# A gated linear recurrence before a squared-relu layer: four edits to the order of a planned kernel

## The chip, the core and the metric

The kernel runs on one core of a Trainium2 chip. Its engines are TensorE (PE, matmuls), VectorE (DVE), ScalarE (ACT), GpSimd (POOL) and SyncE (SP); each has its own queue and works it off in order, and DMA transfers are issued from the queues of SP, ACT and POOL. The metric is the device time of one execution in microseconds.

## What is computed

```python
scale = np.minimum(mag, 0.999) / (mag + 1e-06)      # mag = |a|
for t in range(S):                                   # S = 768, D = 48, 4 batches x 8 heads
    new_re = ar * S_re - ai * S_im
    new_im = ar * S_im + ai * S_re
    S_re, S_im = (new_re + kv, new_im)               # kv = outer(k_t, v_t)
    y[:, :, t] = np.einsum('bhd,bhde->bhe', q[:, :, t], S_re)
x = y.transpose(0, 2, 1, 3).reshape(B * S, H * D)    # 3072 x 384
g = np.maximum(x @ w_in, 0.0) ** 2                   # 384 x 2048
out = g @ w_out                                      # 2048 x 384
```

A complex state of 48 x 48 per batch and head decays by a normalised complex gate at each step, takes in a product of k and v, and is read by q. The result, head by head in a row of 384, goes through two matrices with a squared relu between them.

## The kernel before

The 3072 tokens are worked in six blocks n = 0 to 5 of 512 tokens. A batch has 768 tokens, so blocks 0 and 3 begin with a fresh state, blocks 1 and 4 cross from one batch to the next, and blocks 2 and 5 end one. Eight heads lie in two halves z = 0, 1 of four; a pair is two heads, so a block has four pairs, 0 and 1 in half 0, 2 and 3 in half 1.

Per block the code writes these steps, in functions of `fast_path`:

- `load` (L926): a_re, a_im, q, k of both halves into the tiles `aq0`, `aq1`. For block 0 the a_im parts are issued by ScalarE, a_re, q and k by SP, and half 0 of the gates comes in two parts (u = 0, 1); for the later blocks GpSimd issues all. When a half's gates have landed, GpSimd copies one element (L931) and from then on fetches weights (L821).
- `chain`: `roots` (squares L979/L984, sum L987, logarithm, exponential and square on ScalarE L989 to L994, a Newton step on VectorE L997, L1001), `normalise` (L1007 to L1021) and `inner` (products within four tokens, L1036 to L1041). For block 0 `joint` then turns and sums on TensorE with a permutation and its negative (L1111), and ScalarE copies the result to `e` (L1122, L1125). The negative, `nperm`, lives in the tile `yt0`; ScalarE writes it at L1072. Then VectorE scans over the chunks (L1197 to L1219), TensorE turns the result back (L1090), `factors` and `apply` give every token its own decay (L1129 to L1153, L1320 to L1367). The products of q and k with these factors are written into the tiles `f` (L1365). `gather` moves the K~ rows from there to `KC0` or `KC1` by DMA (L1409).
- `pairs`: for blocks 1 to 5, `turn` transposes f in 32 x 32 blocks on VectorE (L1449) and moves them by 12 DMAs per pair into a `QT` tile (L1454), four of them on ScalarE's queue and eight on SP's; for block 0 TensorE transposes instead (L1473) and ScalarE copies (L1476). `score` multiplies within a chunk on TensorE (L1495), and VectorE masks the result into an `A` tile (L1501; for block 1 also into `T`). `keep` makes chunk states from K~ and v on TensorE (L1525); VectorE copies those with no predecessor (L1535) and adds the others to the state before (L1537) in the tiles `St` and `S`. `mix` puts both together on TensorE (L1549, L1553) into one bank, ScalarE copies it to a `yt` tile (L1559), and SP moves it by DMA to `xT` (L1567).
- `dense`, in two groups of 256 tokens: first matrix (L1609), relu and square on ScalarE (L1641, L1642), second matrix (L1656 in block 0, then L1718 in a form with seven products and additions by VectorE, L1733, L1742, and a copy by ScalarE, L1737).

The weights come as 64-bit floats and are converted in pieces by ScalarE (L834, L838) and VectorE (L840, L844, L847) between these steps in blocks 0 and 1. `sums_of_w2` (L1708) prepares sums of the second matrix for the form with seven products.

The order is set by a planner, the class `Plan`. Each step is added with its engine, an assumed duration, what it reads and writes and a rank; a DMA step has a size and an assumed latency too. `order` simulates: at each moment every engine takes the ready step with the lowest rank. `shift` adds offsets from two tables, by number of group and of step, to the ranks. `emit` writes the instructions in that order and, where it foresees TensorE waiting, fills the time with matmuls of the identity with itself (L739).

Of the kernel before, what the change touches and what calls it, by code (L numbers as in the profile page):

```python
# [632 lines left out]
def fast_path(ctx, tc, q, k, v, a_re, a_im, moe_w_in, moe_w_out, out, flag):  # L633
# [310 lines left out]
    def chain(n):  # L944
# [126 lines left out]
        if n == 0:  # L1071
            step("ACT", 0.25, [], [("yt", 0)], lambda: act.mul(out=nperm, in_=perm, mul=-1.0),  # L1072
                 rank)
        for fn in (roots, normalise, inner):
            for z in range(2):
                fn(z)

# [318 lines left out]
    def gather(n, z, p, np):  # L1396
# [5 lines left out]
        for i in needs(n):  # L1402
            for lo, hi, at in spans(i):
# [7 lines left out]
                    rank, (hi - lo) * np * 2 * R * 4, group=(n, p))  # L1411
# [14 lines left out]
    def pairs(n, which):  # L1426
# [9 lines left out]
        def turn(i):  # L1436
# [13 lines left out]
            for b in range(W):  # L1450
                for j in range(NJ):
# [4 lines left out]
                            in_=T6[32 * b:32 * b + 32, i % 2, j]), rank, 65536,  # L1456
# [49 lines left out]
        def keep(i):  # L1506
# [23 lines left out]

            def go2():
                for j in need:
                    o = new if j == 3 else at[j + 1]
                    if at[j] is None:
                        dve.tensor_copy(out=o, in_=ps[:, j])  # L1535
                    else:
                        dve.tensor_tensor(out=o, in0=ps[:, j], in1=at[j], op=ALU.add)  # L1537
            step("DVE", len(need) * (tt(2 * D) + 0.11) - 0.11, [(b,), ("S", n % 2, i)],
# [319 lines left out]
    for n in range(AFTER):  # L1858
        for j in range(3):
# [4 lines left out]
        groups={5: -99.15, 9: -3.76, 14: 438.99, 15: 438.99, 25: 104.57, 68: -227.0, 70: 100.43, 73:  # L1864
# [5 lines left out]
        single={11: -198.18, 14: 0.04, 51: -1.52, 52: 4.52, 58: -215.58, 96: 438.99, 143: 438.99,  # L1870
# [66 lines left out]
```

## Time and profile before

| | us |
|---|---|
| median of 3 runs (680.1 to 682.59) | 681.67 |
| profiled execution | 678.34 |
| its span, first to last instruction | 676.6 |
| TensorE busy | 656.4 |
| VectorE busy | 557.2 |
| ScalarE busy | 341.8 |
| mean granted TensorE clock | 0.994 of full |

A row of the timeline gives start, duration, engine, line, operation, the tile written and read, and in brackets the idle time just before and what ended it. ACTq and SPq are rows of a queue that issues DMAs; how long such a row lasts is how long the queue was held. A row of waits gives what waited for what: total, times, longest. A row of windows gives a stretch and its length, then busy time and instructions of PE, PEld, DVE, ACT and POOL, then the granted clock, the share of the DMA engines and GB/s.

### The profile page before, as it was taken

How to read it: one execution, taken by the hardware profiler on the slowest of the kernel's cores; microseconds unless marked ns; L12 is line 12 of the kernel's file. 1: busy time of each engine (PE TensorE's matmuls, PEld its weight loads, DVE VectorE, ACT ScalarE, POOL GpSimd, SP SyncE). 2: the span in 40 equal slices, each digit the busy share in tenths (PEclk: the TensorE clock that was granted, in tenths of full speed). 3: DMA queues.
4: the chain of work that ended last, by engine and by line, in shares of the span. 5: the costliest groups of instructions: out<-in, count | busy, mean ns of one | idle time of the engine just before them, and what ended most of it. 6: DMA issues, size and time to landing. Idle time of an engine off the chain costs nothing.

```text
span 676.6 us, 13669 instructions
## 1 busy us (share of the span) xinstructions
PE 656.4 (97%) x5194; PEld 593.0 (88%) x5194; DVE 557.2 (82%) x1153; ACT 341.8 (51%) x564; POOL 147.5 (22%) x247
## 2 busy tenths in 40 slices
PE   9989979999989999999999999999999999999996
PEld 9989868768768898998988998989899999989996
DVE  4999998899599999989998898999987995247641
ACT  5997588954366524557425639236548132132230
POOL 4400455033210012013133143031050110042100
PEclk9989999999989999999999999999999999999999
DMA  7941596235850018525156443166260264187600
GB/s 224 318 159 36 131 232 205 89 94 146 210 149 25 23 43 202 141 73 141 36 135 165 123 118 69 48 161 171 68 176 24 50 151 108 40 301 263 222 8 23
DMA packets 39492, 86.33 MB, mean 128 GB/s; under 512 B 8917, under 2 KB 16545, under 8 KB 39417
## 3 DMA queue, kind: packets, MB, share of 16 engines
q0 software_dynamic: 16576, 57.03, 29.9%
q1 hardware_dynamic: 17784, 22.20, 12.7%
q10 hardware_dynamic: 5056, 6.13, 3.5%
q8 instruction: 43, 0.70, 0.5%
q14 instruction: 33, 0.26, 0.1%
HBM read 48.76 MB, written 4.72 MB: 79 GB/s over the span
## 4 chain that ended last, share of the span: by engine, by line
PE 59%; DVE 8%; issue 1%; DMA 1%; ACT 1%; ACTq 0%; DVEq 0%
PE d L1609 26%; PE d L1718 23%; PE sc L1495 3%; PE yp L1549 2%; PE yp L1553 2%; PE tr L1525 2%; DVE g L1733 1%; DMA QT<-aq 1%; DVE T L1708 1%; DVE f L1365 1%; PE tr L1090 0%; DVE f L1036 0%; DVE KC L1217 0%; DVE aq L1449 0%; DVE aq L1067 0%
## 5 line engine op out<-in xcount | busy, mean ns | idle before, releaser
L1609 PE MATMUL d<-xT,w 128*128 128x256 f32 x1104 | 245.9, 380 | 2.9 <-DMA xT<-yt 2.1
L1609 PEld LDWEIGHTS d<-xT,w 128*128 128x128 f32 x1104 | 208.0, 190 | 32.5 <-DMA xT<-yt 2.5
L1641 ACT ACTIVATE g<-d 128x512 f32<-128x512 f32 x92 | 54.7, 595 | 180.5 <-PE d L1609 112.7
L1718 PE MATMUL d<-w,g 128*128 128x192 f32 x640 | 112.3, 328 | 1.6 <-ACT ot L1737 1.6
L1718 PEld LDWEIGHTS d<-w,g 128*128 128x128 f32 x640 | 104.4, 190 | 3.3 <-ACT ot L1737 2.1
L1718 PE MATMUL d<-T,g 128*128 128x192 f32 x480 | 85.3, 327 | 0.3 <-DVE g L1733 0.3
L1733 DVE TENSOR_TENSOR g<-g 128x512 f32<-128x512 f32 x80 | 54.2, 686 | 31.7 <-PE d L1718 17.0
L1718 PEld LDWEIGHTS d<-T,g 128*128 128x128 f32 x480 | 79.0, 190 | 1.5 <-DVE g L1733 0.6
L1642 ACT ACTIVATE g<-g 128x512 f32<-128x512 f32 x96 | 60.6, 631 | 3.1
L739 PE MATMUL d<-ident 128*128 128x128 f32 x502 | 59.7, 283 | 1.6 <-POOL ident masks.py:199 1.6
L739 PEld LDWEIGHTS d<-ident 128*128 128x128 f32 x502 | 58.9, 199 | 2.0 <-POOL ident masks.py:199 1.6
L1679 POOL DMA_DIRECT2D out_dram<-ot x22 | 12.5, 567 | 196.3 <-DVE ot L1742 184.9
L1449 DVE STREAM_TRANSPOSE aq<-f 128x768 f32<-128x768 f32 x40 | 47.9, 1266 | 0.2
L1559 ACT COPY yt<-yp 112x512 f32<-112x512 f32 x24 | 26.5, 1106 | 40.0 <-PE yp L1553 34.4
L1409 POOL DMA_DIRECT2D KC<-f x56 | 34.7, 626 | 53.0 <-issue 22.0
L1365 DVE TENSOR_TENSOR f<-aq 128x768 f32<-128x768 f32 (+1 forms) x56 | 44.3, 839 | 0.4
L1656 PE MATMUL d<-w,g 128*128 128x384 f32 x128 | 44.0, 491 | 0.3 <-DVE w L847 0.3
L1742 DVE TENSOR_TENSOR ot<-ot,d 128x192 f32<-128x192 f32 x70 | 23.6, 349 | 18.3 <-PE d L1718 17.7
L1495 PE MATMUL sc<-QT 96*64 96x64 f32 (+1 forms) x736 | 38.1, 252 | 0.0
L1656 PEld LDWEIGHTS d<-w,g 128*128 128x128 f32 x128 | 23.7, 190 | 15.3 <-DVE w L847 0.9
L1495 PEld LDWEIGHTS sc<-QT 96*64 96x64 f32 x736 | 35.0, 137 | 0.4 <-issue 0.2
L1036 DVE TENSOR_TENSOR f<-aq 128x768 f32<-128x768 f32 (+1 forms) x48 | 34.2, 755 | 0.6
(198 smaller groups left out, 955.5 us busy)
## 6 DMA issues: line engine op xcount, KB each, us to landing
QT<-aq SPq DMA_DIRECT2D x152, 64.0 KB, 2.2
f<-in_moe_w_in_dram POOLq DMA_DIRECT2D x8, 768.0 KB, 6.9
f<-in_moe_w_out_dram POOLq DMA_DIRECT2D x8, 768.0 KB, 6.9
QT<-aq ACTq DMA_DIRECT2D x76, 64.0 KB, 2.7
out_dram<-ot POOLq DMA_DIRECT2D x22, 192.0 KB, 3.1
KC<-f POOLq DMA_DIRECT2D x20, 192.0 KB, 4.3
xT<-yt SPq DMA_DIRECT2D x36, 96.0 KB, 2.3
T<-in_moe_w_out_dram POOLq DMA_DIRECT2D x4, 768.0 KB, 9.7
```

The source lines that it names most:

```text
L739: plan = Plan(lambda b: pe.matmul(bank[b][:, 0:C], lhsT=ident, rhs=ident, start=True, stop=True), ["d2", "d1", "d0"], lambda ap: tc.nc.val ...
L1036: dve.tensor_tensor(out=f, in0=x0, in1=x1[:, j].unsqueeze(1).to_broadcast(list(x0.shape)), op=ALU.mult)
L1365: lambda j=j, r=r, o=o: dve.tensor_tensor(out=o[:, :, :, r * D:(r + 1) * D], in0=qk[:, j], in1=a[:, r], op=ALU.mult), late[z])
L1409: lambda i=i, queue=queue, lo=lo, hi=hi, a0=a0, a1=a1: queue.dma_start(out=kc[lo:hi, i], in_=nat[a0:a1]),
L1449: lambda nat=nat, dst=dst, j=j: dve.transpose(out=dst[:, j], in_=nat), rank)
L1495: pe.matmul(sa[r:r + C // 2, j, :, lo:32], lhsT=T[:, j, 1, h, ts(late, C // 2)], rhs=T[:, j, 0, h].rearrange("p (c t) -> p c t", c=W)[:, : ...
L1609: pe.matmul(ps, lhsT=w1[:, f // FP, m, ts(f % FP, C)], rhs=xT[:, n % 2, m, ts(grp, G)], start=(m == 0), stop=(m == NM - 1))
L1641: act.activation(out=o, in_=ps, func=AF.Relu)
L1642: act.activation(out=o, in_=o, func=AF.Square)
L1656: pe.matmul(ps, lhsT=gt[:, f % 2, ts(i, C)], rhs=w2[:, f], start=(f == 0), stop=(f == NF - 1))
L1718: pe.matmul(bank[b][:, 0:DH], lhsT=g4[:, r, j], rhs=w(j), start=first and j == 0, stop=last and j == NT - 1)
L1733: step("DVE", tt(4 * C), gk(x0, h) + gk(x1, h), gk(o, h), lambda: dve.tensor_tensor(out=g4[:, o, sl], in0=g4[:, x0, sl], in1=g4[:, x1, sl] ...
```

## The change

Four edits:

1. In block 0 ScalarE's negation of the permutation is no longer written first in the chain, but behind `normalise` of half 0; it waits there for two columns of that half's `f`.
2. In `keep`, chunk states with no predecessor (16 copies, in blocks 0, 1, 3 and 4) are copied from the accumulator by ScalarE (L1533 of the new file) instead of VectorE. VectorE's additions now also wait for `St`, that is for these copies.
3. The planner counts 2.7 us instead of 1.8 for the landing of K~ rows, and 2.2 instead of 1.8 for that of QT.
4. The two tables of `shift` are replaced as a whole.

```diff
-        if n == 0:
-            step("ACT", 0.25, [], [("yt", 0)], lambda: act.mul(out=nperm, in_=perm, mul=-1.0),
-                 rank)
         for fn in (roots, normalise, inner):
             for z in range(2):
                 fn(z)
+                if n == 0 and z == 0 and fn is normalise:
+                    step("ACT", 0.25, key(0, 1), [("yt", 0)], lambda: act.mul(
+                        out=nperm, in_=perm, mul=-1.0), rank)
...
                         out=kc[lo:hi, i], in_=nat[a0:a1]),
-                    rank, (hi - lo) * np * 2 * R * 4, group=(n, p))
+                    rank, (hi - lo) * np * 2 * R * 4, 2.7, group=(n, p))
...
                             out=t[32 * j:32 * j + 32, b],
-                            in_=T6[32 * b:32 * b + 32, i % 2, j]), rank, 65536,
+                            in_=T6[32 * b:32 * b + 32, i % 2, j]), rank, 65536, 2.2,
...
+            begun = [j for j in need if at[j] is None]
+            for j in begun:
+                step("ACT", 0.27, [(b,)], [("St", s)], lambda j=j: act.copy(
+                    out=at[j + 1], in_=ps[:, j]), rank, group=(n, i))
+
             def go2():
                 for j in need:
-                    o = new if j == 3 else at[j + 1]
-                    if at[j] is None:
-                        dve.tensor_copy(out=o, in_=ps[:, j])
-                    else:
+                    if j not in begun:
+                        o = new if j == 3 else at[j + 1]
                         dve.tensor_tensor(out=o, in0=ps[:, j], in1=at[j], op=ALU.add)
-            step("DVE", len(need) * (tt(2 * D) + 0.11) - 0.11, [(b,), ("S", n % 2, i)],
+            step("DVE", (len(need) - len(begun)) * (tt(2 * D) + 0.11) - 0.11,
+                 [(b,), ("S", n % 2, i), ("St", s)],
...
-        groups={5: -99.15, 9: -3.76, 14: 438.99, 15: 438.99, 25: 104.57, 68: -227.0, 70: 100.43, 73:
+        groups={3: -342.38, 5: -305.58, 7: -355.32, 9: -326.37, 14: 448.38, 15: 448.29, 24: 1.52,
```

What this does to the order, at three places. The first is the start of ScalarE's queue in block 0; `yt_89` holds the negative permutation, `aq_68` and `aq_69` are the halves 0 and 1 of the gates, a DMA of 128x2x192 is one of the two parts of half 0. Before and then after:

```order
L667 ACT_TABLE_LOAD
L1072 ACTIVATE yt_89<-perm 128x128
L926 DMA aq_68<-in_a_im_dram 128x2x192 x2
L926 DMA aq_69<-in_a_im_dram 128x4x192
L979 ACTIVATE f_70<-aq_68 128x384 x2
```

```order
L667 ACT_TABLE_LOAD
L926 DMA aq_68<-in_a_im_dram 128x2x192
L926 DMA aq_69<-in_a_im_dram 128x4x192
L926 DMA aq_68<-in_a_im_dram 128x2x192
L979 ACTIVATE f_70<-aq_68 128x384
```

The negation is gone from the front, and the second part of half 0 has moved behind the whole of half 1. On VectorE, from the inner products of half 0 on (L1041), two L840, one L847 and one L1067 stood ahead of the last L1036 of half 1, which `joint` waits for, and now stand behind it.

The second place is VectorE in block 1, where the f of half 1 is done (L1365) and the first mix of the block needs its masks (L1501, into T and A_85) and its states (St_87). Before and then after; the additions of L1537 are L1540 in the new file:

```order
L1365 TENSOR_TENSOR f_71<-aq_69 128x4x4x48 x4
L1537 TENSOR_TENSOR St_87<-tr_112,S_84 96x96
L1535 COPY St_87<-tr_112 96x96
L1537 TENSOR_TENSOR S_83<-tr_112,St_87 96x96
L1501 TENSOR_TENSOR T<-sc_110,mask 128x512
L1501 TENSOR_TENSOR A_85<-sc_111,mask 128x512
L1449 STREAM_TRANSPOSE aq_69<-f_71 128x4x2x3x32 x4
```

```order
L1365 TENSOR_TENSOR f_71<-aq_69 128x4x4x48 x4
L1449 STREAM_TRANSPOSE aq_69<-f_71 128x4x2x3x32 x3
L1501 TENSOR_TENSOR T<-sc_110,mask 128x512
L1501 TENSOR_TENSOR A_85<-sc_111,mask 128x512
L1449 STREAM_TRANSPOSE aq_69<-f_71 128x4x2x3x32
L1540 TENSOR_TENSOR St_87<-tr_112,S_84 96x96
L1540 TENSOR_TENSOR S_83<-tr_112,St_87 96x96
```

Three of the four transposes of half 1 have moved ahead of the masks and the fourth ahead of the additions, and the copy has left the queue. Further on in this block, the masks of pair 2 have moved: one stands ahead of L997 and the other behind L1001, and both ahead of L1708, where they stood behind all of these and behind the state additions.

The third place is ScalarE in block 1, at the same time: QT_73 and QT_74 are the QT tiles of pairs 2 and 3, whose issues come from the transposes above; L964 to L1007 is the chain of the next block; L1559 is L1563 in the new file and L1641, L1642 are L1645, L1646. Before and then after:

```order
L1454 DMA QT_73<-aq_69 32x512 x4
L964 ACTIVATE f_70,sums<-aq_68 128x1536
L1559 COPY yt_89<-yp 112x4x4x32
L1454 DMA QT_74<-aq_69 32x512 x4
L989 ACTIVATE f_70<-f_70 128x768
L991 ACTIVATE f_70<-f_70 128x768
L994 ACTIVATE f_70,sums<-f_70 128x768
```

```order
L1454 DMA QT_73<-aq_69 32x512 x4
L1533 COPY St_87<-tr_112 96x96
L1645 ACTIVATE g<-d_109 128x512
L1646 ACTIVATE g<-g 128x512
L1645 ACTIVATE g<-d_107 128x512
L1646 ACTIVATE g<-g 128x512
L1454 DMA QT_74<-aq_69 32x512 x2
L1533 COPY St_88<-tr_113 96x96
L1454 DMA QT_74<-aq_69 32x512 x2
L964 ACTIVATE f_70,sums<-aq_68 128x1536
L1563 COPY yt_89<-yp 112x4x4x32
L989 ACTIVATE f_70<-f_70 128x768
```

The four issues of QT_74 have moved ahead of L964 and of the copy to yt, and the copies of the new states stand behind QT issues. Elsewhere: at the end of block 0 the K~ gathers of half 1 have moved ahead of block 1's loads on GpSimd and ahead of the xT moves on SP, `keep` of pair 3 stands before the mix of pair 2 on TensorE, and its state additions stand before the last masks on VectorE. In block 3 eight QT issues in a row stand before a relu on ScalarE, where there were five. The last rows of each engine are as before.

More of the change, by code (lines that the diff above doesn't have):

```diff
@@ L1863, in fast_path @@
     plan.shift(
-        groups={5: -99.15, 9: -3.76, 14: 438.99, 15: 438.99, 25: 104.57, 68: -227.0, 70: 100.43, 73:
[5 rows of a table removed]
-        single={11: -198.18, 14: 0.04, 51: -1.52, 52: 4.52, 58: -215.58, 96: 438.99, 143: 438.99,
[10 rows of a table removed]
+        groups={3: -342.38, 5: -305.58, 7: -355.32, 9: -326.37, 14: 448.38, 15: 448.29, 24: 1.52,
[7 rows of a table added]
+        single={3: 97.06, 11: -213.0, 44: 41.06, 48: -1.3, 49: 26.15, 53: 32.15, 63: 1.44, 65: 2.25,
[20 rows of a table added]
     with tc.manual_schedule():
```

42 rows, old and new, of tables (groups, single) are left out of this document.

## The prediction

> **What bounds the kernel now.** I read the page's first part, then the waits of TensorE, then the stages in which those waits lie.
>
> ```profile
> span 676.6 us, 13669 instructions
> PE 656.4 (97%) x5194; PEld 593.0 (88%) x5194; DVE 557.2 (82%) x1153; ACT 341.8 (51%) x564; POOL 147.5 (22%) x247
> ...
> L739 PE MATMUL d<-ident 128*128 128x128 f32 x502 | 59.7, 283 | 1.6 <-POOL ident masks.py:199 1.6
> ```
>
> TensorE is busy for 97% of the span, but 59.7 us of that is L739, the matmuls of the identity with itself that the planner puts into waits it foresees. They all lie in the first 95 us, before the first dense block, so the start is bounded by something else, and only from about 100 us on is TensorE the bound. The profiled execution took 678.34 us: 676.6 of span and 1.74 outside it. The sum below is made against it; the median of the runs shown, 681.67, lies 3.33 above it, and I carry that distance over unchanged.
>
> What is left of TensorE's time outside the start is in its waits (total, times, longest).
>
> ```profile
> PE yp L1549 <- DVE A L1501: 2.6, 2, 2.0
> PE d L1609 <- DMA xT<-yt: 2.1, 1, 2.1
> PE tr L1111 <- DVE f L1036: 1.7, 1, 1.7
> ...
> PE d L1718 <- ACT ot L1737: 1.6, 1, 1.6
> PE tr L1525 <- DMA KC<-f: 1.6, 2, 1.4
> PE d L1609 <- ACT g L1641: 0.8, 1, 0.8
> ```
>
> No wait is longer than 2.1 us. The waits for L1036, for KC<-f and for xT<-yt lie before 100 us. Those for A (L1501), for ot (L1737) and for g (L1641) lie behind, and each of those is lost for good, since nothing catches it up. Two of the waits cost more than their length. The stages by windows show it in the granted clock (the number ahead of the DMA share):
>
> ```profile
> 30.00:40.00 10.00, 8.26 (x82) 7.54 (x80) 9.76 (x14) 9.89 (x11) 1.76 (x3) 0.86 1.03 299
> ...
> 90.00:100.00 10.00, 6.57 (x107) 5.73 (x104) 9.11 (x15) 7.91 (x10) 3.41 (x6) 1.00 1.05 251
> ...
> 190.00:200.00 10.00, 9.65 (x116) 8.02 (x118) 9.16 (x15) 7.04 (x11) 2.04 (x3) 0.83 0.54 145
> ...
> 470.00:480.00 10.00, 8.38 (x92) 8.01 (x88) 9.30 (x15) 6.19 (x9) 0.80 (x2) 1.00 0.62 166
> ```
>
> The stages with the gaps of 1.71 us (34.5) and 1.95 us (188.3) lost 14% and 17% of 10 us, that is 1.4 and 1.7 us of full speed. The stages with gaps of 2.08 and 1.62 us kept 1.00. So a gap of this size throttles sometimes, and its price is its length or its length plus about 1.7.
>
> **The change, part by part: the start (0 to 100 us).** ScalarE's first rows are:
>
> ```profile
> 2.27 0.31 ACT L1072 ACTIVATE yt<-perm 128x128 f32<-128x128 f32 x1 [0.16 <-POOL perm L722]
> 2.27 2.43 ACTq L926 DMA_DIRECT2D aq<-in_a_im_dram  x3
> ...
> 6.82 0.56 DVE L984 TENSOR_TENSOR f<-aq 128x384 f32<-128x384 f32 x1 [5.33 <-DMA aq<-in_a_im_dram]
> ...
> 10.42 0.56 DVE L984 TENSOR_TENSOR f<-aq 128x384 f32<-128x384 f32 x1 [2.37 <-DMA aq<-in_a_im_dram]
> ```
>
> The table load ends at 2.10; the negation and the first a_im transfer start at 2.27, and VectorE then idles 5.33 and 2.37 us for a_im. With the negation gone from the front, the three issues can begin 0.17 us sooner. They also change places: the whole of half 1 goes ahead of the second part of half 0. The second part was needed at 10.42, and half 1 landed last, at 12.81:
>
> ```profile
> 12.81 0.22 POOL L931 COPY gate<-aq 128x1 f32<-128x1 f32 x1 [1.78 <-DMA aq<-in_a_im_dram]
> ...
> 29.54 0.55 DVE L840 TENSOR_SCALAR w<-KC 128x768 uint32<-128x768 uint32 x1
> ...
> 30.01 0.95 DVE L847 CUSTOM_DVE_ANT_0 w<-w,w 128x1536 uint16<-128x1536 uint16 x1
> ...
> 36.20 0.32 PE L1111 MATMUL tr<-perm,f 128*64 128x128 f32 x1 [1.71 <-DVE f L1036]
> ...
> 36.53 0.76 DVE L1067 TENSOR_TENSOR aq<-aq,f 128x576 f32<-128x576 f32 x1
> ```
>
> VectorE's order loses what stood ahead of the end of half 1's inner products (L1036, which released L1111 at 36.20): two L840, one L847 and one L1067 now stand behind it, 2 x 0.55 + 0.95 + 0.76 = 2.8 us. That is the most there is to gain. The other end: the queue carries the same bytes, so the part of half 0 that is now last may land when half 1 did, at 12.81, which is 2.4 us later than it was used; then 0.4 is left. The negation itself (0.31 us, now behind normalise of half 0) is first read by L1111, which waits for half 1's products anyway, and costs nothing as long as they end later. I take 2.0, nearer to VectorE's work, because in the rows its idle time ends at 11 us and from there to 36 us it has work.
>
> This reaches the first dense matmul only if the end of the start moves too:
>
> ```profile
> 91.84 1.28 DVE L1501 TENSOR_TENSOR A<-sc,mask 128x512 f32<-128x512 f32 x2
> ...
> 93.40 0.40 PE L1525 MATMUL tr<-v,KC 128*64 128x48 f32 x8 [1.35 <-DMA KC<-f]
> ...
> 95.27 0.65 PE L1549 MATMUL yp<-A,v 128*48 128x128 f32 x8
> ...
> 99.73 0.45 PE L1609 MATMUL d<-xT,w 128*128 128x256 f32 x1 [2.08 <-DMA xT<-yt]
> ```
>
> Block 0's last masks were done at 93.12. Its last mix began at 95.27, since the keep of pair 3 waited 1.35 us for K~ rows and its state adds came behind that. In the new order the last K~ gathers go out ahead of block 1's loads, the keep of pair 3 stands before the mix of pair 2, and the adds stand before the last masks. So the mix now waits for the masks alone. The 2.8 us of pushed work come back between the first products of the scan and those masks, less four St copies of 0.244 (below): 1.8 of the 2.0 won above are spent again, and the masks end near 92.9. With half a microsecond for what else the mix reads, it begins near 93.4, **1.9 us** sooner. If K~ rows still land last, 0; if the masks profit in full, 3.5.
>
> **Block 1's pairs (160 to 204 us).**
>
> ```profile
> 180.49 2.79 ACTq L1454 DMA_DIRECT2D QT<-aq  x2
> 183.33 0.84 ACT L989 ACTIVATE f<-f 128x768 f32<-128x768 f32 x1 [4.26 <-DMA QT<-aq]
> ...
> 186.05 0.96 DVE L997 SCALAR_TENSOR_TENSOR f<-f 128x768 f32<-128x768 f32 x1 [5.78 <-ACT f L994]
> ...
> 189.41 1.27 DVE L1501 TENSOR_TENSOR A<-sc,mask 128x512 f32<-128x512 f32 x2
> ...
> 190.23 0.90 PE L1549 MATMUL yp<-A,T 128*48 128x128 f32 x3 [1.95 <-DVE A L1501]
> ```
>
> This is a chain through three engines. ScalarE was held in its queue by QT issues, so L989 began at 183.33; VectorE, in order, waited 5.78 us for L994; the masks stood behind L997, L1001, L1708 and the state adds, and so TensorE waited 1.95 us and ran slow after. In the new order all four of these QT issues stand ahead of L964 and yt, and one mask stands ahead of L997, the other right behind L1001. The masks then no longer depend on L1708 or the adds, 0.95 + 0.7 us, and L989 is not behind an issue. I take the whole away: 1.95 + 1.7 = **3.65** (at worst nothing, if the issues block as long at their new place).
>
> Against it stands the first mix of the same block:
>
> ```profile
> 165.34 3.56 DVE L1365 TENSOR_TENSOR f<-aq 128x768 f32<-128x768 f32 x4
> ...
> 168.59 4.14 PE L1656 MATMUL d<-w,g 128*128 128x384 f32 x12
> ...
> 170.04 0.68 DVE L1501 TENSOR_TENSOR A<-sc,mask 128x512 f32<-128x512 f32 x1
> 170.64 4.75 DVE L1449 STREAM_TRANSPOSE aq<-f 128x768 f32<-128x768 f32 x4
> ...
> 173.13 3.27 ACTq L1454 DMA_DIRECT2D QT<-aq  x4
> ```
>
> The masks were done at 170.72 and TensorE was busy until 172.73, a margin of 2.0 us. Now three of the four transposes (4.75 / 4 = 1.19 us each) stand before these masks and the fourth before the adds: 4.75 us later, less a copy of 0.24, overruns the margin by 2.5. Beside it ScalarE's copy of the state stands behind four QT issues, which can begin after two transposes: 168.9 + 2.4 + 3.3 + 0.3 = 174.9, the same size. Both are lessened by VectorE's copies that are gone (four of block 0, 1.0 us) and by idle time of VectorE on its way there, which earlier inputs may fill. Its longest idle time between 100 and 172 us:
>
> ```profile
> DVE f L1018 <- ACT f L1016: 2.2, 1, 2.2
> ```
>
> I take **+1.0**, with 0 and 2.5 + 1.7 = 4.2 as ends.
>
> **The rest.**
>
> ```profile
> L1535 DVE COPY St<-tr x16: 229/244/255, 73.9 to 487.4; 96x96 f32<-96x96 f32 x16
> ```
>
> Sixteen copies of 0.244 us leave VectorE, 3.9 us, and go to ScalarE, which is busy for 51%. Behind 100 us VectorE isn't the bound, so this is 0 by itself; what counts is that an add now waits for ScalarE, whose queue is held by QT issues, before relu (L1641) alone 29.1 us in nine waits, as ScalarE's waits show, with one such issue from its rows:
>
> ```profile
> ACT g L1641 <- DMA QT<-aq: 29.1, 9, 5.8
> ```
>
> ```profile
> 350.86 3.25 ACTq L1454 DMA_DIRECT2D QT<-aq  x5
> ```
>
> In block 3 eight QT issues now stand in a row before a relu where there were five: at 3.25 / 5 = 0.65 each, 2.0 us more on top of the wait of 0.82, and at most 1.7 of slow clock. The later waits of 0.82 and 1.62 could also go. I take 0, between -2.4 and +3.7. The longer latencies of K~ rows and QT are numbers of the planner and cost nothing on the chip. The tail behind 670 us has the same rows.
>
> Sum: -1.9 - 3.65 + 1.0 + 0 = -4.55. Profiled 673.8; beside the median, **677.1 us**.
>
> **A rule weighed.** The rows above show half speed after gaps of 1.71 and 1.95 us. The Trainium skill, "TensorE: Matmul & The Clock Gate", Part 1: The HAM clock gate, gives the cold clock only after at least one idle window of about 3.4 us. By that rule no gap here would throttle, the one at 188.3 would be worth 1.95, and the sum -2.85, 678.8 us; the clock of 0.83 right behind it speaks against that.
>
> **The rivals.** A measurement of this kernel tells a change of about 0.5% (3.4 us) from none.
> - The stall of block 1 moves instead of going: the first mix loses 4.2, the start wins 0.4. -0.4 - 3.65 + 4.2 = +0.15: 681.8. For it: transposes ahead of the masks in VectorE's order; against it: the 2.2 us of VectorE's idle time.
> - The change of a_im's places brings nothing, as the queue's bytes are the same: -0.4 - 3.65 + 1.0 = -3.05: 678.6. For it: 12.81 is when the last byte landed.
> - Slower: ScalarE's queue becomes the bound. St copies and relus stand behind QT issues and hold VectorE's adds, and with them the mix. It decides from an overhang above the 2.0 us of margin. First mix of block 1 4.2 instead of 1.0, relu of block 3 +3.7: 677.1 + 6.9 = 684.0; with half a QT issue (1.6) and slow clock (1.7) at pair 1 of block 1, 687.3. For it: 29.1 us of such waits now; against it: most copies in blocks 3 and 4 stand ahead of the issues, not behind.
>
> **How the numbers follow.** Forecast 0.50; nothing from a_im 0.17, half of it past 0.5%; the stall moves 0.18; the gap without slow clock 0.02; slower 0.13. Faster 0.58, same 0.29, slower 0.13. The range's low end takes the start at 3.5, no loss at the first mix and the later waits gone: 681.67 - 3.5 - 3.65 - 2.4 = 672.1, so 672.0; the high end takes in the slower case with two of its places, 684.0.
>
> **What would show it.** Right: L1111 released near 34 instead of 36.2; first L1609 that waits for xT near 97.8; no wait of L1549 for A near 186; a clock of 1.00 there. Wrong: a wait of L1549 for St or A near 171 over 2 us with a clock near 0.8 behind it; a wait of L1609 for g in block 3 over 2 us; a first dense matmul at 99 or later.

## The result, and the profile after

The changed kernel takes **686.04 us** (median of ten runs, 683.72 to 687.69) against 682.30 for the kernel before on the same chip (680.1 to 683.17). The ratio is 1.0054, with a 95% interval of 1.0036 to 1.0071: slower by about half a per cent, where 677.1 was predicted. The profiled execution took 684.40, 6.06 more than the one before; the medians differ by 3.7, since the profiled execution of before (678.34) lies below all its timed ones.

The page's first part and TensorE's waits of the changed kernel (from L1549 on its lines lie four behind those of before: L1609 is L1613, L1641 is L1645, L1656 is L1660, L1549 is L1553, L1718 is L1722):

```profile
span 682.7 us, 13643 instructions
PE 658.3 (96%) x5188; PEld 594.5 (87%) x5188; DVE 552.7 (81%) x1137; ACT 344.9 (51%) x580; POOL 147.2 (22%) x247
```

```profile
PE d L1613 <- DMA xT<-yt: 5.7, 1, 5.7
PE d L1660 <- ACT g L1646: 2.1, 1, 2.1
PE sc L1495 <- issue: 2.0, 1, 2.0
PE d L1613 <- DVE ot L1746: 1.8, 1, 1.8
...
PE d L1613 <- ACT g L1645: 1.1, 1, 1.1
```

TensorE's busy time hardly differs (658.3 for 656.4). What differs is one wait of 5.7 us for xT, where the longest of before was 2.1, and three behind it of about 2. The waits for A (L1501), for KC<-f and of L1111 for f have left the top of the list, so much of what was forecast did happen. The windows show what the new waits cost beside their length:

```profile
96.00:98.00 2.00, 0.38 (x1) 0.41 (x2) 1.97 (x3) 1.97 (x4) 0.00 (x0) 0.50 0.98 192
98.00:100.00 2.00, 2.00 (x6) 1.53 (x6) 2.00 (x3) 2.00 (x3) 0.00 (x0) 0.50 0.13 26
...
160.00:170.00 10.00, 7.87 (x25) 5.05 (x24) 9.86 (x15) 1.66 (x3) 4.04 (x6) 0.85 0.78 186
...
180.00:190.00 10.00, 7.34 (x63) 5.14 (x61) 3.10 (x6) 3.28 (x5) 2.03 (x3) 0.88 0.85 216
190.00:200.00 10.00, 10.00 (x124) 8.52 (x121) 7.76 (x11) 8.00 (x13) 1.50 (x2) 0.78 0.64 166
```

In the second row TensorE is busy all the time and runs at 0.50. From 160 on, three stretches lie at 0.85, 0.88 and 0.78; before, only one did (0.83 from 190 on), and the stage from 160 to 180 had neither gap nor slow clock. Two rows of before:

```profile
160.00:170.00 10.00, 10.00 (x86) 7.54 (x85) 9.83 (x20) 3.46 (x6) 4.03 (x6) 1.00 0.73 185
...
180.00:190.00 10.00, 8.28 (x98) 5.84 (x96) 4.15 (x8) 5.41 (x9) 1.49 (x2) 1.00 0.84 215
```

Where the time went, from the gaps of TensorE and the times at half clock (a granted clock of 0.50) in both traces (half clock is counted with half its length, from where work goes on):

| us | before | after | difference |
|---|---|---|---|
| last mix of block 0, which the prediction followed, begins | 95.27 | 89.58 | -5.7 |
| wait for xT behind it | 2.08 | 5.67 | +3.6 |
| half clock behind that | 0 | 2.3 | +2.3 |
| gaps from there to 250 us | 2.9 | 5.6 | +2.7 |
| half clock there | 1.7 | 5.1 | +3.4 |
| gaps behind 250 us | 2.4 | 2.9 | +0.5 |
| sum | | | +6.8 |

The sum is 0.7 above the measured 6.06; the ends of matmuls are modelled, so the gaps are not exact to a tenth. Another count of the same two traces compares the dense matmuls of the first matrix with the same number: the 17th begins 0.2 us late, the 351st (259 us into the kernel before) 5.2, the 1101st 6.3. Both say where to look: **the start won 5.7 us and lost them all at once, and block 1 lost 5 to 6 more.**

The start of the changed kernel in the timeline, and the row of before that answers to the last one:

```profile
0.82 1.28 ACT L667 ACT_TABLE_LOAD   x1 [0.82 <-PEq L1937]
0.86 1.57 ACTq L926 DMA_DIRECT2D aq<-in_a_im_dram  x3
...
4.04 0.56 DVE L984 TENSOR_TENSOR f<-aq 128x384 f32<-128x384 f32 x1 [2.55 <-DMA aq<-in_a_im_dram]
...
7.87 0.56 DVE L984 TENSOR_TENSOR f<-aq 128x384 f32<-128x384 f32 x1 [0.99 <-DMA aq<-in_a_im_dram]
...
34.91 0.35 DVE L1197 TENSOR_TENSOR KC<-e 128x192 f32<-128x192 f32 x1
```

```profile
41.05 0.35 DVE L1197 TENSOR_TENSOR KC<-e 128x192 f32<-128x192 f32 x1
```

ScalarE's queue now issues a_im at 0.86, while the table load is still running, and not at 2.27 behind the negation. VectorE gets the data at 4.04 and 7.87 instead of 6.82 and 10.42, and the scan begins 6.1 us sooner. Then comes the end of block 0:

```profile
82.75 1.50 POOL L926 DMA_DIRECT2D aq<-in_q_dram  x2
...
88.22 1.28 DVE L1501 TENSOR_TENSOR A<-sc,mask 128x512 f32<-128x512 f32 x2
...
89.58 0.65 PE L1553 MATMUL yp<-A,v 128*48 128x128 f32 x8
...
97.62 1.62 PE L1613 MATMUL d<-xT,w 128*128 128x256 f32 x3 [5.67 <-DMA xT<-yt]
```

```profile
88.41 1.30 POOL L926 DMA_DIRECT2D aq<-in_q_dram  x2
```

The masks end at 89.50 and the mix begins at 89.58: it waits for the masks alone. But from the mix to the dense matmul that waits it is 8.04 us where it was 4.46. GpSimd issues block 1's eight transfers of q and k from 82.75 on, 5.7 us sooner than before (88.41). The three small moves to xT (32, 96 and 64 KB) that the dense block waits for go out from 87.5 on (91.3 before); seven of the eight loads are under way ahead of them, where it was four. By the semaphores in the traces these three land 8.9 to 9.8 us after their issue, where they took 7.7 to 8.0 before. So they start 3.7 us sooner and not 5.7, and are then 1.2 to 1.8 us longer under way; both together make the wait longer. They carry the mix before the last, not the last one, which the prediction followed. Nothing in GpSimd's queue ties those loads to xT. Behind the wait stands more: the relus on ScalarE wait for the dense matmuls, L1016 of the next block's chain waits behind the relus, and VectorE waits for L1016:

```profile
109.96 0.96 DVE L1018 SCALAR_TENSOR_TENSOR f<-f 128x768 f32<-128x768 f32 x1 [7.00 <-ACT f L1016]
```

Then block 1 in the changed kernel:

```profile
159.80 3.59 ACTq L1454 DMA_DIRECT2D QT<-aq  x3
163.48 1.42 ACTq L1454 DMA_DIRECT2D T<-aq  x2
...
164.95 0.60 ACT L1645 ACTIVATE g<-d 128x512 f32<-128x512 f32 x1 [4.52 <-DMA QT<-aq]
...
166.26 2.17 PE L1660 MATMUL d<-w,g 128*128 128x384 f32 x4 [2.13 <-ACT g L1646]
...
181.07 5.73 ACTq L1454 DMA_DIRECT2D QT<-aq  x2
...
186.90 1.48 ACT L964 ACTIVATE f<-aq 128x1536 f32<-128x1536 f32 x1 [6.63 <-DMA QT<-aq]
...
187.20 1.60 PE L1495 MATMUL sc<-QT 96*64 96x128 f32 x16 [1.96 <-issue]
...
189.50 0.45 PE L1553 MATMUL yp<-A,T 128*48 128x128 f32 x1 [0.70 <-ACT yt L1563]
```

Rows of ACTq are ScalarE's own queue held by the issuing of transfers. A relu stands behind three of them into QT and two into T, and TensorE waits 2.13 us for it. L964 stands behind two that took 5.73, nearly all of it waiting: by its semaphore the second could begin only when a move that SP had issued at 180.04 had landed, at 186.21. The copy to yt stands behind L964, and TensorE waits for the copy. The scores wait 1.96 us; the profile puts this down to "issue", but the semaphores they wait for are those of moves to QT, which land at that time. The wait for A at 188.3, which was to go, has gone; these three stand in its place.

### The profile page after: what moved, and what is told of

It is laid out like the page before. It is cut to its first block, busy times and chain, and to the rows that moved or that the text cites. A ratio compares the mean times of both kernels' runs of the same rounds, so it can differ in the third digit from the quotient of the medians.

```text
span 682.7 us, 13643 instructions
## 1 busy us (share of the span) xinstructions
PE 658.3 (96%) x5188; PEld 594.5 (87%) x5188; DVE 552.7 (81%) x1137; ACT 344.9 (51%) x580; POOL 147.2 (22%) x247
## 4 chain that ended last, share of the span: by engine, by line
PE 67%; DVE 18%; DMA 6%; ACT 3%; issue 2%; SPq 0%; ACTq 0%; DVEq 0%
PE d L1613 30%; PE d L1722 25%; DMA QT<-aq 4%; PE sc L1495 3%; PE yp L1553 3%; PE yp L1557 2%; DVE f L1365 2%; DVE f L1036 2%; PE tr L1525 2%; DMA xT<-yt 2%; PE d L1660 2%; DVE f L1337 1%; DVE aq L1449 1%; DVE aq L1021 1%; DVE w L847 1%
## 5 line engine op out<-in xcount | busy, mean ns | idle before, releaser
L1613 PE MATMUL d<-xT,w 128*128 128x256 f32 x1104 | 250.6, 384 | 8.7 <-DMA xT<-yt 5.7
L1613 PEld LDWEIGHTS d<-xT,w 128*128 128x128 f32 x1104 | 209.8, 192 | 41.3 <-issue 7.0
L1645 ACT ACTIVATE g<-d 128x512 f32<-128x512 f32 x92 | 54.8, 596 | 184.6 <-PE d L1613 119.9
L1722 PE MATMUL d<-w,g 128*128 128x192 f32 x640 | 111.5, 327 | 0.0
L1722 PEld LDWEIGHTS d<-w,g 128*128 128x128 f32 x640 | 104.8, 190 | 0.9 <-issue 0.2
L1722 PE MATMUL d<-T,g 128*128 128x192 f32 x480 | 85.5, 327 | 0.0
L1722 PEld LDWEIGHTS d<-T,g 128*128 128x128 f32 x480 | 78.9, 190 | 0.9 <-issue 0.4
L1646 ACT ACTIVATE g<-g 128x512 f32<-128x512 f32 x96 | 60.6, 631 | 3.1
L1660 PE MATMUL d<-w,g 128*128 128x384 f32 x128 | 44.8, 496 | 2.9 <-ACT g L1646 2.1
L1563 ACT COPY yt<-yp 112x512 f32<-112x512 f32 x24 | 26.7, 1113 | 38.6 <-PE yp L1557 38.6
L1365 DVE TENSOR_TENSOR f<-aq 128x768 f32<-128x768 f32 (+1 forms) x56 | 44.3, 839 | 0.7
L1495 PE MATMUL sc<-QT 96*64 96x64 f32 (+1 forms) x736 | 39.8, 256 | 2.0 <-issue 2.0
L1660 PEld LDWEIGHTS d<-w,g 128*128 128x128 f32 x128 | 23.8, 190 | 17.8 <-ACT g L1646 2.7
L1036 DVE TENSOR_TENSOR f<-aq 128x768 f32<-128x768 f32 (+1 forms) x48 | 34.2, 753 | 0.4
```

Of the source, the lines that this page charges most:

```text
L1036: dve.tensor_tensor(out=f, in0=x0, in1=x1[:, j].unsqueeze(1).to_broadcast(list(x0.shape)), op=ALU.mult)
L1365: lambda j=j, r=r, o=o: dve.tensor_tensor(out=o[:, :, :, r * D:(r + 1) * D], in0=qk[:, j], in1=a[:, r], op=ALU.mult), late[z])
L1495: pe.matmul(sa[r:r + C // 2, j, :, lo:32], lhsT=T[:, j, 1, h, ts(late, C // 2)], rhs=T[:, j, 0, h].rearrange("p (c t) -> p c t", c=W)[:, : ...
L1613: pe.matmul(ps, lhsT=w1[:, f // FP, m, ts(f % FP, C)], rhs=xT[:, n % 2, m, ts(grp, G)], start=(m == 0), stop=(m == NM - 1))
L1645: act.activation(out=o, in_=ps, func=AF.Relu)
L1646: act.activation(out=o, in_=o, func=AF.Square)
```

## The experiments

Eight of the twelve edits are made where the order is handed to the emission, by moving single steps: a pair (n, m) puts step n right behind step m. So a moved step takes its instructions and its transfers along, and everything else keeps its place. For all runs the kernel before was timed on the same chip, and the ratio is to it.

### The loads of q and k behind xT, in the changed kernel

The eight loads of block 1 go behind GpSimd's copy of one element out of xT (L1851), which waits for the moves to xT.

```diff
         order = self.order()
+        for n, m in [(472, 331), (473, 472), (474, 473), (476, 474), (478, 476), (479, 478), (477, 479), (475, 477)]:
+            order.remove(n)
+            order.insert(order.index(m) + 1 if m is not None else 0, n)
```

> The changed kernel, with one move in GpSimd's queue: block 1's eight q and k loads stand behind the copy of one element of xT (L1851 of the changed file), so they start only when xT of block 0 has landed. Theory A (the start is won, but xT's moves share the DMA engines with these loads, so the first dense block waits 5.67 us, runs slow after it, and VectorE, whose L1018 stands behind relus that wait for the dense block, idles 7.0 us and carries block 1's pairs late): the wait of L1613 for xT falls under 1.5 us, the first dense matmul that waits starts near 92.5 instead of 97.6, VectorE's idle time before L1018 falls under 3 us, and the stalls between 160 and 190 us (2.13 and 1.96) shrink with it: 672 to 678 us. Theory B (xT's moves are slow by themselves, held by SP's queue): the wait stays above 4 us, 685 to 687. Theory C (the stalls of block 1 come from QT issues on ScalarE and have nothing to do with the late start): only the start's 5 to 8 us come back, the stalls at 164 and 185 stay: 678 to 681.

Measured: 678.68 us, ratio 0.9955 [0.9933, 0.9977]; the changed kernel has 1.0054 [1.0036, 1.0071], so the place of these eight loads is worth 1.0%, about 6.7 us. Two rows of its timeline:

```profile
92.48 2.86 PE L1613 MATMUL d<-xT,w 128*128 128x256 f32 x12
...
98.52 0.19 POOL L1851 COPY gate<-xT 128x3 f32<-128x3 f32 x1 [14.51 <-DMA xT<-yt]
```

The dense block starts at 92.48 and does not wait; VectorE's 7.00 us ahead of L1018 are gone too. The ninth dense matmul begins 6.0 us sooner than in the changed kernel, and the last one still does by 5.8, so nothing of it was given back. By the semaphores in the traces, the three moves that the dense block needs land 2.0 to 2.9 us after their issue here; in the changed kernel, beside seven loads, it took 8.9 to 9.8. The Trainium skill, "DMA: Bandwidth & Descriptors", section "Queues, rings and completion order", says that a DMA engine serves the queues that have work in turn, a packet at a time; these landing times with and without the loads agree with that.

The part of the theory that made block 1's stalls a consequence of this wait fell:

```profile
PE sc L1495 <- issue: 2.9, 1, 2.9
PE yp L1553 <- ACT yt L1563: 1.7, 1, 1.7
PE d L1660 <- ACT g L1646: 1.4, 1, 1.4
PE sc L1495 <- DMA T<-aq: 1.1, 1, 1.1
```

Seven microseconds of waits stand in block 1 without any wait for xT ahead of it. The time is that of Theory C.

### The negation alone, in the kernel before

```diff
         order = self.order()
+        for n, m in [(58, 86)]:
```

Step 58 is the negation, 86 the L1016 of half 0; nothing else of the change is in.

> The kernel before, with edit 1 alone: the negation stands behind L1016 of half 0 on ScalarE, all else in the order of before. Theory A: the three a_im issues begin at 0.86 us instead of 2.27 and the scan starts 2 to 3 us sooner, but at the end of block 0 K~ rows and xT's moves stay bound by the DMA engines, so the first dense matmul moves by less than 1.5: 681 to 683 us (before 682.3). Rival (what the start wins reaches the end): 679 to 680.

Measured: 678.38 us, 0.9954 [0.9936, 0.9971].

```profile
0.86 1.53 ACTq L926 DMA_DIRECT2D aq<-in_a_im_dram  x3
...
38.35 0.36 DVE L1197 TENSOR_TENSOR KC<-e 128x192 f32<-128x192 f32 x1
...
97.06 3.91 PE L1609 MATMUL d<-xT,w 128*128 128x256 f32 x10 [2.68 <-DMA xT<-yt]
```

One instruction of 0.31 us, moved, brings 0.46%: the issues begin at 0.86, the scan 2.7 us sooner (38.35 for 41.05), and the first dense matmul that waits as much (97.06 for 99.73). So by the medians edit 1 alone is a gain that reaches the end, as the rival had it; Theory A, by which little of it would arrive, is out. In this one trace half clock follows the wait for xT (from 96.71 to 100.12), and from the 13th dense matmul on 1.2 of the 2.7 us are left; what else makes up the difference of the medians is not shown. The other 3.4 us by which the changed kernel's scan is early appear when the new order is added; the next experiment shows what that order wins without edit 1.

### The negation first again, in the changed kernel

```diff
         order = self.order()
+        for n, m in [(88, None)]:
```

> The changed kernel with edit 1 undone and the order kept otherwise: the negation stands first on ScalarE, ahead of the a_im issues. The scan starts 1.5 to 3 us later than 34.9. Theory A: the wait for xT takes this up (5.67 becomes 3 to 4.5 us), the first dense matmul moves by less than 1 us: 684 to 687. Rival (every us of the start counts): 687.5 to 689.

Measured: 691.19 us, 1.0139 [1.0107, 1.0170].

```profile
2.27 2.61 ACTq L926 DMA_DIRECT2D aq<-in_a_im_dram  x3
...
13.21 0.56 DVE L984 TENSOR_TENSOR f<-aq 128x384 f32<-128x384 f32 x1 [0.17 <-DMA aq<-in_a_im_dram]
...
40.37 0.36 DVE L1197 TENSOR_TENSOR KC<-e 128x192 f32<-128x192 f32 x1
...
103.42 1.19 PE L1613 MATMUL d<-xT,w 128*128 128x256 f32 x2 [5.96 <-DMA xT<-yt]
```

The scan is 5.5 us later, the dense block 5.8, and the wait for xT is as long as before (5.96 for 5.67). I had thought that part of what the start loses would be taken up by that wait. It is not: the loads move with the start, and so the wait comes along. The start's loss counts in full here, and under the new order the negation's place is worth 0.85%, more than under the old one. The new order alone brings the scan forward by no more than 0.7 us (40.37 for 41.05): with the negation first, the second part of half 0, which the change put last, reaches VectorE at 13.21, where it was 10.42 before and is 7.87 with the whole change.

### The states copied by VectorE again

```diff
-                step("ACT", 0.27, [(b,)], [("St", s)], lambda j=j: act.copy(
-                    out=at[j + 1], in_=ps[:, j]), rank, group=(n, i))
+                step("ACT", 0.27, [(b,)], [("St", s)], lambda: None,
+                     rank, group=(n, i))
...
-                    if j not in begun:
+                    if j in begun:
+                        dve.tensor_copy(out=at[j + 1], in_=ps[:, j])
+                    else:
```

> The changed kernel with edit 2 undone and the order kept: VectorE copies the 16 states with no predecessor, directly ahead of its additions, and ScalarE copies none. Theory A: the place of the copies is of no weight; 685 to 687 us, same stalls. Rival (VectorE's additions held by ScalarE's queue make block 1's stalls): the waits between 160 and 190 us shrink, 681 to 684.

Measured: 687.82 us, 1.0106 [1.0082, 1.0131], with the same stalls as the changed kernel (5 us for xT, the rest in block 1). Giving the copies back to VectorE doesn't help; if anything it costs 0.5%. In the traces 1.5 of 2.3 us of it lie ahead of the first dense matmul that waits (99.08 for 97.62); why is not settled. So edit 2 is not what made the kernel slower.

### The order of the start and the order of the rest, apart

Three kernels take one file's order up to the last move to xT of block 0, and the other's behind it, written out as a list of the changed kernel's steps (the fillers are fixed with it):

```diff
-        order = self.order()
+        self.order()
+        order = [0, 1, 113, 114, 5, 2, 3, 4, 58, 59, 60, 61, 75, 62, 66, 63, 6, 67, 68, 64, 69, 7, 11, 74, 21, 70, 8, 71, 12, 76,
...
+        self.fill = {101: (122, 'd2'), 126: (44, 'd2'), 129: (3, 'd2'), 203: (69, 'd2'), 209: (2, 'd2'), 327: (8, 'd2')}
```

The first has the new start, the old rest, and the loads held behind xT.

> The changed code (edits 1 to 3) with the changed order up to the last xT move of block 0, the order of before from there on, and block 1's q and k loads behind xT as in e1. Theory A2 (two causes: the loads ahead of xT at the end of block 0, and, apart from that, the changed order of block 1's pairs): no wait for xT over 1 us, and in block 1 only the stall of before (about 2 us behind 180), 671 to 675 us. Rival D (block 1's stalls come from an early start, whatever the order): stalls of over 5 us between 150 and 190, 676 to 680.

Measured: 676.46 us, 0.9934 [0.9909, 0.9959]. TensorE's waits and the first dense matmul that waits:

```profile
PE d L1722 <- ACT ot L1741: 2.1, 1, 2.1
```

```profile
97.70 0.67 PE L1613 MATMUL d<-xT,w 128*128 128x256 f32 x2 [0.33 <-DMA xT<-yt]
```

No wait in block 1 reaches 1.0; even the 1.95 us for A that the old order has in the kernel before is 0.74 here. So Rival D, whose time this median would fit, is out: its stalls are not there. The median lies 1.5 above the expected range, the profiled run (674.55) inside it; in its trace a wait for ot at 472 us, 1.62 in the kernel before, has grown to 2.13 and drawn half clock behind it.

The second is the old start (negation first) with the new rest.

> The changed code with the order of before up to the last xT move of block 0 (the negation first, too) and the changed order from there on. Theory A2: the stalls of the changed kernel in block 1 (before a L1660, before scores and before a mix, 4 to 9 us with slow clock) stand behind an old start: 684 to 689 us. Rival D: block 1 like before, 681 to 683.

Measured: 684.68 us, 1.0056 [1.0036, 1.0077].

```profile
PE d L1660 <- ACT g L1646: 2.1, 1, 2.1
PE d L1613 <- DMA xT<-yt: 1.7, 1, 1.7
PE yp L1553 <- ACT yt L1563: 1.5, 1, 1.5
...
PE sc L1495 <- issue: 1.1, 1, 1.1
```

The new order of block 1 and behind costs 4.0 us by itself, with a wait for xT no longer than before. In the trace that wait did draw half clock (from 99.02), worth 1.7, but the dense matmuls lose another 4.0 between the 31st and the 351st, that is in block 1. Rival D, by which the new order does no harm under an undisturbed start, is refuted.

The third is the first, with the loads where the change put them.

> As the first of this call, but the q and k loads where the change put them. Theory A2: the wait for xT of 5 us and the slow clock behind it come back, and only they: 5 to 8 us above the first, 677 to 681. If the wait for xT needs the changed order behind it as well, less than 3 us above the first.

Measured: 682.77 us, 1.0006 [0.9984, 1.0029]. The wait for xT is back with 5.28 us, and the median is 6.3 above the first, as expected, though 1.8 outside the range of times that was given. In the trace the 13th dense matmul begins 0.2 us sooner than in the kernel before: the start's gain is gone by then. So the new start is worth nothing as it stands, 0.7% with the loads held; and 0.06% for the start and 0.56% for the rest agree, within the noise, with the 0.54% of the change.

What the new rest costs beside the old one differs with the setting. The right column is of block 1 alone, from one trace each: by how much more the dense matmuls fall behind between the 31st and the 351st.

| start and loads | new rest dearer, whole kernel | in block 1 |
|---|---|---|
| old start | 4.0 us | 4.0 us |
| new start, loads where the change put them | 0.48%, 3.3 us | 4.9 us |
| new start, loads held | 0.21%, 1.4 us (intervals overlap) | 4.5 us |

Block 1 loses 4 to 5 us in all three. With the new start the old rest gives some of that back behind 470 us, where it has the wait for ot (2.95 and 2.13) with its half clock, which the new rest does not have.

### The loads held, in the kernel before

```diff
         order = self.order()
+        for n, m in [(468, 327), (469, 468), (470, 469), (471, 470), (472, 471), (473, 472), (474, 473), (475, 474)]:
```

> The kernel before with one move: block 1's q and k loads stand behind the copy of one element of xT (L1847). Theory A2: its wait for xT of 2.08 us falls under 0.7 and VectorE's idle time before L1018 (2.2) shrinks: 2 to 3.5 us under before. Rival (the loads didn't hold xT in before): within 1 us of before, or slower where block 1 then waits for q and k.

Measured: 677.71 us, 0.9943 [0.9921, 0.9965]. The wait of 2.08 us for xT is gone and its dense matmul begins at 97.57 instead of 99.73. The three moves take 4.4 to 5.3 us instead of 7.7 to 8.0. The kernel before had the same fault on a smaller scale.

### Three attempts at block 1

All three start from the changed kernel with the loads held (678.68). The first moves the two T issues of ScalarE (649, 652) behind the relu that TensorE waited for (434).

```diff
+        for n, m in [(472, 331), (473, 472), (474, 473), (476, 474), (478, 476), (479, 478), (477, 479), (475, 477), (649, 434), (652, 649)]:
```

> The e1 kernel (changed order, loads held) with two T issues of block 1 moved behind the next relu on ScalarE. In e1 that relu waited for QT issues and TensorE for it (1.44 us before L1660 at 158). Theory F (ScalarE's queue, held by issues, makes the stall at 158): it falls under 0.4, and what is behind it moves up by as much: 1.0 to 1.5 us under e1 (ratio to before 0.9933 to 0.9942 where e1 had 0.9955). Rival: the stalls behind take it up; same as e1 within 0.5.

Measured: 677.38 us, 0.9935 [0.9912, 0.9959]. The gap ahead of L1660 shrinks from 1.44 to 0.18: it was those issues that held the relu. But the scores that need T then wait longer (2.54 us instead of 1.08), and in the traces the 351st dense matmul begins within 0.1 us of where it did: what was won is paid back there. The medians show 0.2% less, as Theory F expected, but their intervals overlap, so a gain is not shown.

The second moves pair 3's four QT issues behind L964 and the copy to yt (661).

```diff
+        for n, m in [(472, 331), (473, 472), (474, 473), (476, 474), (478, 476), (479, 478), (477, 479), (475, 477), (702, 661), (705, 702), (708, 705), (711, 708)]:
```

> The e1 kernel with the four QT issues of pair 3 of block 1 moved back behind L964 and the copy to yt on ScalarE, as they stood in before. In e1 ScalarE was held 6.7 us by these issues, L964 and the copy came after, and a mix waited 1.73 us for the copy and ran slow. Theory F: that stall and its slow clock go, 2 to 3.4 us under e1 (0.9905 to 0.9925). Rival G (the scores of pair 3 wait for QT's moves anyway, and now longer, as a third of them starts later): the wait before L1495 grows from 2.94 to over 4, within 1 us of e1.

Measured: 676.50 us, 0.9920 [0.9889, 0.9951].

```profile
180.00:190.00 10.00, 9.55 (x156) 7.94 (x158) 6.34 (x10) 8.14 (x12) 1.95 (x3) 1.00 0.74 175
```

The wait for yt (1.73) and the half clock behind it are gone; this stretch, at 0.83 with the loads held alone, runs at 1.00, and the scores of pair 3 do not wait longer for it (2.06 for 2.94). So it was the queue, held by these issues, that held yt. In the traces the 351st dense matmul begins 2.5 us sooner; the intervals of the two ratios overlap, so in time the gain is likely rather than shown.

The third moves block 2's gate loads of half 0 (854, 853) behind its q and k, to free the transfers that QT shares the engines with.

```diff
+        for n, m in [(472, 331), (473, 472), (474, 473), (476, 474), (478, 476), (479, 478), (477, 479), (475, 477), (854, 858), (853, 854)]:
```

> The e1 kernel with block 2's a_im and a_re loads of half 0 moved behind its q and k loads in GpSimd's queue, so that they start only when QT's moves of half 0 are read. Theory G (QT's moves of pairs 2 and 3, started sooner by the transposes that stand ahead of the masks, now share the DMA engines with these 768 KB): the waits before L1495 (1.07 and 2.94) fall under 1 in sum, the copy to yt comes sooner, and 3 to 5 us are won against e1 (ratio 0.988 to 0.991). Rival F (the issue queue of ScalarE): within 1 us of e1.

Measured: 678.66 us, 0.9964 [0.9944, 0.9984], no change.

The waits of the scores fall from 1.07 + 2.94 us to 1.52, so the loads of the next block do hold QT in part; but the waits for yt and g grow by 0.5 each (to 2.2 and 1.9), and half clock in this block from 3.4 us to 10.2. What else holds those moves stays open.

### The two moves that won, together, in the kernel before

```diff
+        for n, m in [(58, 86), (468, 327), (469, 468), (470, 469), (471, 470), (472, 471), (473, 472), (474, 473), (475, 474)]:
```

> The kernel before with two moves and nothing else: the negation behind L1016 of half 0 (as in e2), and block 1's q and k loads behind the copy of one element of xT (as in b1). If the two causes add up (-2.9 and -3.0): 674 to 676, ratio 0.990 to 0.993. If one takes up the other: 677 to 678.

Measured: **673.97 us**, 0.9893 [0.9857, 0.9928], the fastest of all and faster than both kernels.

```profile
37.99 0.35 DVE L1197 TENSOR_TENSOR KC<-e 128x192 f32<-128x192 f32 x1
...
93.20 2.86 PE L1609 MATMUL d<-xT,w 128*128 128x256 f32 x12
```

The scan is 3.1 us early, the dense block does not wait for xT, and the two gains (0.46% and 0.57%, together 1.03%) add up: 1.07% was measured.

## Why the prediction was wrong

Forecast 677.1 (672 to 684), a gain; measured 686.04, a loss. By its own steps:

- **The start, -1.9: right in direction, too small by far, and then lost.** "The three issues can begin 0.17 us sooner" was the mis-sized term. I took the table load's end, 2.10, for the earliest moment; the issues in fact begin at 0.86, beside it, 1.41 us sooner, and the scan began 6.1 us sooner rather than the 2.0 taken: 2.7 by the negation alone, 0.7 by the order alone, the rest only by both. The worry that half 0's second part would be late was right as long as the negation stands first (13.21 for 10.42), and with the early issues it fell away (7.87).
- **"So the mix now waits for the masks alone": right.** 89.50 and 89.58. The mix began 5.7 us sooner where the upper end was 3.5.
- **From the mix to the dense block: the step that is missing.** The prediction carried the mix's gain to the first dense matmul as if the moves to xT took as long as before, though it had seen the row of 2.08 us and that the last K~ gathers go out "ahead of block 1's loads". It never asked when those loads go out themselves. Nor did it see that the 2.08 us ended with moves issued at 91.27 and just after, ahead of the last mix at 95.27: it is the mix before the last that they carry. The loads come 5.7 us sooner, since GpSimd's queue holds them behind nothing that the dense block needs, and they make xT late: 8.9 to 9.8 us to land, 5.67 us of wait and 2.3 of half clock. Held back, the same start is worth 0.7% (676.46 against 682.77 and a ratio of 1.0006). None of the rivals had this. That the first dense matmul that waits begins at 97.62, where "near 97.8" was named as a sign of being right, is luck: a gain of 5.7 less 3.6 of longer wait, and the half clock right behind it takes the rest.
- **Block 1's stall, -3.65: the wait for A went, its time did not.** The step that failed is "I take the whole away", argued from the masks alone. Its worst case was "nothing, if the issues block as long at their new place"; they block longer (5.73 us for two, where a row of two took 2.79), and other instructions stood behind them. Exchanging the rest of the order puts it at +4.0 us under the old start, +3.3 under the new and +1.4 with the loads held, with what lies behind block 1 in it, and at 4 to 5 us in block 1 alone, where -2.65 was forecast for both terms of block 1: the largest error of the sum.
- **The first mix of block 1, +1.0: not there.** It did not wait for masks or states. The stall near that place is another, 2.13 us for a relu at 164, and a relu behind issues the sum had only for block 3.
- **The St copies, 0: right**, by 0.5% rather a gain.
- **The rest, 0: right.** 2.44 us of gaps became 2.91 (counted by the dense matmuls, the stages behind block 1 lose 1.1). In block 3 the row of eight issues and the relu behind it came as forecast, and cost 1.09 instead of 0.82, not 2.8:

```profile
352.30 7.23 ACTq L1454 DMA_DIRECT2D QT<-aq  x8
...
360.23 1.99 PE L1613 MATMUL d<-xT,w 128*128 128x256 f32 x8 [1.09 <-ACT g L1645]
...
408.21 1.99 PE L1613 MATMUL d<-xT,w 128*128 128x256 f32 x8 [1.82 <-DVE ot L1746]
```

- **The rival on the other side, "ScalarE's queue becomes the bound", 684.0 to 687.3, chance 0.13:** its time was the one that came, and for block 1 its mechanism in kind, though through the relu and yt, not through St. That its time fits is in part luck: it has the loss in block 1 by much the right way, but it keeps the start's 1.9 us and has the first mix and block 3 for what xT took. It set against itself that most copies in blocks 3 and 4 stand ahead of the issues; the relu and the copy to yt in block 1, which stand behind them, it did not follow.
- **Half clock.** "A gap of this size throttles sometimes" held, and the last section says when.
- **The signs.** None of the three signs of being wrong came: no such wait near 171, 1.09 us for g in block 3, a first dense matmul at 97.62. Of those of being right, L1111 came even sooner (31.46, without a wait) and only the clock of 1.00 near 186 failed. The signs watched the places that the sum had, and the loss came at two that it did not have.

## What to carry to other kernels

A step that goes sooner takes with it every transfer that waits for nothing but a free tile: before booking a gain, look for the loads of the next stage in the queues and ask what small move on the path they will now run beside. Hold such loads behind the arrival of what the path waits for; a copy of one element is enough, and here it brought 0.6% in the kernel before, without any other change. And where an engine both computes and issues transfers, a stall that is taken out of it can come back at whatever stands behind the issues; count the queue's rows, not the engine's busy share.

## What the runs showed of the hardware

- ScalarE's queue issued transfers at 0.86 while the table load ran from 0.82 to 2.10; behind an ACTIVATE in the same queue, which waited for GpSimd's permutation until then, the first issue came at 2.27, and three took 2.43 to 2.61 us instead of 1.53 to 1.57. In the kernel before the second and third of them begin at 3.40 and 4.09, each after a wait for a semaphore of an earlier transfer, which the early ones did not have.
- Half clock begins on a fixed grid. In each of the 14 traces of this study the starts of stretches at half clock lie whole multiples of 3.413 us apart (before: 37.23 and 190.83, 45.0 of them), and I counted TensorE's gaps by cells of that grid:

| idle time in a cell | cells at full clock | half clock in the next cell |
|---|---|---|
| 1.85 us or more | 23 | 23 |
| 1.61 to 1.84 | 18 | 5 |
| 0.5 to 1.60 | 91 | 0 |

So the 2.08 us at 97.64 in the kernel before cost only their length, since they lay across a border of the grid (98.67, 18 cells behind 37.23), 1.03 and 1.05, while the 1.95 at 188.28 lay in one cell. The Trainium skill, "TensorE: Matmul & The Clock Gate", Part 1: The HAM clock gate, states a free-running window of 3413 ns, and the traces agree; it asks for an idle window, and here about half a window's idle time was enough.
- At half clock less is enough to stay there: the nine cells at half clock with 0.70 us of idle time or more (six of them with 0.70 to 1.99) were all followed by another, three with 0.35 to 0.52 were not. The gap of 0.70 at 188.80 in the changed kernel lay in the cell behind the 1.96, and half clock lasted 6.83 us there, 1.7 us more of cost.
